# Attention visits of batch 1 half a step to a whole step later, in the middle of FFN steps and in the output steps

## The chip, the cores and the metric

One core of one Trainium2 chip. The metric is the device time of one execution in microseconds (us), the median over executions. Engines are named as in the profile: PE (TensorE matmul), PEld (its weight loads), DVE (VectorE), ACT (ScalarE), POOL (GpSimd), SP (SyncE, which here issues DMAs).

Where a time is compared with the kernel before, the ratio is the mean time of one kernel's runs over that of the other's of the same rounds, so it is not quite the ratio of the medians that are quoted.

## The reference, cut to what matters

```python
# attention with k and v projected from 1024 to 64 positions; 8 batches, 8 heads, head_dim 64
k_proj = einsum('ks,bhsd->bhkd', E, k);  v_proj = einsum('ks,bhsd->bhkd', F, v)
attn = softmax(q @ k_proj.T / sqrt(64)) ;  x = attn @ v_proj        # then heads are joined
# FFN on the 8192 x 512 tokens
h = maximum(maximum(x @ w1, x @ w2), x @ w3)                          # 512 -> 768
out = h @ w_out                                                       # 768 -> 512
```

## The kernel before

A batch is worked in two halves (`ch`, 512 tokens). One half is six FFN steps (`up`: three weights of four matmuls each give three PSUM banks, the tile `banks` into which PE writes its results; their maximum becomes one slice of `hT`) and four output tiles (`down`). PE always works on the FFN of batch b; the attention of batch b+1 is slipped in between steps as "visits", by a plan. The kernel is emitted in the written order on every engine, so the plan decides not only when PE does a visit but also where its Exp and Ln stand among the FFN's own ACT and DVE work.

```python
def two():    # two neighbouring PSUM banks; bank() deals one. The bank that a clock model says is free first
    ...
def sc(b, g):         # scores of a pair of heads: PE now, Exp on ACT at the next run_later()
    def f():
        t = scores(b, g, lo, nsi)
        later.append(lambda: exps(b, g, lo, nsi, t))

def za(b, g, then=False):        # PE: sums, values; ACT: Ln, then Exp(-x); DVE: xT = values * that
    def f():
        z = sums(b, g, lo, nsi)
        av = values(b, g, lo, nsi)
        invert(b, g, lo, nsi, z)             # zl = Ln (frees the sums' banks), zi = Exp
        ...
        scale_x(b, g, lo, nsi, av)           # xT
...
def up(b, ch, jt):
    h, done = [], []
    early = jt == 0
    for i in range(3):
        h.append(bank())
        up_mm(h[i][0], i, b, ch, jt, range(NCT - early))
        done.append(clock["pe"])
    ...
    h1s = ffn_sb.tile([P, CHUNK], FP32, name="h1s")
    nc.scalar.copy(out=h1s, in_=h[0][0])                       # ACT
    r = runs("s", done[0], 0.6, h[0][1])
    run_later()
    m12 = ffn_sb.tile([P, CHUNK], FP32, name="m12")
    nc.vector.tensor_tensor(out=m12, in0=h[1][0], in1=h1s, op=ALU.max)   # DVE
    runs("v", max(r, done[1]), 0.69, h[1][1])
    most(hTs[b, ch][:, jt, :], *h[2], m12)                     # DVE: hT
...
# plan of batch 0 (its visits are of batch 1), second half: (half, step); 6 to 9 are the output tiles
(1, 0): [kproj(1)],
(1, 1): [kt(1)],
(1, 2): [sc(1, 0), sc(1, 1), vproj(1), ld(2)],
(1, 3): [za(1, 0), sc(1, 2)],
(1, 4): [za(1, 1), sc(1, 3)],
(1, 5): [za(1, 2)],
(1, 7): [za(1, 3)],
...
for step in range(NJT):
    up(b, ch, step)
    behind(ch, step)           # the visits of (ch, step)
for tt in range(SPC):
    down(b, ch, tt, ...)
    behind(ch, NJT + tt)
```

`qT` of batch 1 is made by two DMA transposes issued on SP; the scores read it. The loads of k and v of batch 1 are issued by POOL near 24 and 26 us.

The softmax here doesn't subtract the row's maximum and nothing guards it: scores larger than these inputs give would overflow.

Of the kernel before, what the change touches and what calls it, by code (L numbers as in the profile page):

```python
# [15 lines left out]
def kernel(  # L16
# [62 lines left out]
    def bank():  # L79
        n = min(range(8), key=lambda n: free[n])  # L80
        deal((n,))
        return psum_t[:, n, :], (n,)
# [110 lines left out]
    def scores(b, g, lo, nsi):  # L193
        t, ns = two()
        n = nsi // 2
        for c in range(2):
            for hp in range(2):
                rows = slice(hp * HALF, (hp + 1) * HALF)
                at = g * SI + lo + c * n
                nc.tensor.matmul(  # L200
                    out=t[c * HALF:(c + 1) * HALF, hp, 0:n * P],
                    lhsT=kpTs[b][rows, g, :],
                    rhs=qTs[b][rows, at:at + n, :],
                    start=True, stop=True,
                )
        return t[:, :, 0:n * P], ns, pe(n * MM / 4 + 0.1)

    def exps(b, g, lo, nsi, sc):
        t, ns, ready = sc
        pTs[b, g, lo] = att.tile([P, 2, CHUNK], BF16, name="pT", bufs=4)[:, :, 0:nsi * HALF]  # L210
        nc.scalar.activation(out=pTs[b, g, lo], in_=t, func=AF.Exp, scale=scale)  # L211
        runs("s", ready, 0.17 + nsi * 0.107, ns)
# [14 lines left out]
    def sums(b, g, lo, nsi):  # L227
        return pair_mm(b, g, lo, nsi, lambda rows, hp: ones[rows])

    def invert(b, g, lo, nsi, z):  # L230
        t, ns, ready = z
        zl = att.tile([P, 2, CHUNK], FP32, name="zl", bufs=1)[:, :, 0:nsi * HALF]
        nc.scalar.activation(out=zl, in_=t, func=AF.Ln)  # L233
        runs("s", ready, 0.17 + nsi * 0.107, ns)
        if nsi == SI:
            zi = att.tile([P, 2, CHUNK], FP32, name="zi", bufs=2)
        else:
            zi = att.tile([P, 2, CHUNK // 2], FP32, name="zi0", bufs=4)
        nc.scalar.activation(out=zi, in_=zl, func=AF.Exp, scale=-1.0)  # L239
        zis[b, g, lo] = zi, runs("s", ready, 0.17 + nsi * 0.107)  # L240

    def values(b, g, lo, nsi):
        if b not in xTs:
            xTs[b] = att.tile([P, NCT, SI, P], BF16, name="xT")
        return pair_mm(b, g, lo, nsi, lambda rows, hp: vps[b][rows, 2 * g + hp, :])

    def scale_x(b, g, lo, nsi, av):
        t, ns, ready = av
        zi, when = zis.pop((b, g, lo))
        nc.vector.tensor_tensor(  # L250
            out=xTs[b][:, g, lo:lo + nsi, :].rearrange("a (c s) p -> a c (s p)", c=2),
            in0=t, in1=zi, op=ALU.mult,
        )
        runs("v", max(ready, when), 0.17 + nsi * 0.13, ns)
# [8 lines left out]
    def sc(b, g, lo=0, nsi=SI):  # L263
# [3 lines that stand above are left out]
        return f  # L267

    def za(b, g, lo=0, nsi=SI, then=False):
# [3 lines that stand above are left out]
            invert(b, g, lo, nsi, z)  # L273
            if then:
                later.append(lambda: scale_x(b, g, lo, nsi, av))
            else:
                scale_x(b, g, lo, nsi, av)
        return f
# [84 lines left out]
    def vproj(b):  # L363
        def f():
            t, ns = bank()
            proj(b, 2, t, (LO, HI), 4 * D)

            vps[b] = att.tile([P, H, D], BF16, name="vp")
            for hh, hs in enumerate((LO, HI)):
                i = t[hh * HALF:(hh + 1) * HALF, 0:4 * D].rearrange("a (h d) -> a h d", d=D)  # L370
                for to in range(2):
                    copy("sv"[hh], vps[b][to * HALF:(to + 1) * HALF, hs, :], i, ns, 0.4)
        return f
# [161 lines left out]
                most(hs[:, jt] if i == 1 else hTs[0, 0][:, jt, :], *h[jt], hs[:, jt])  # L535
                then((i, jt))

    def up(b, ch, jt):
        if jt == 0:
            hTs[b, ch] = ffn_sb.tile([P, NJT, CHUNK], BF16, name="hT")  # L540
        h, done = [], []
        early = jt == 0
        for i in range(3):
            h.append(bank())
            up_mm(h[i][0], i, b, ch, jt, range(NCT - early))
            done.append(clock["pe"])
        if early:
            for i in range(3):
                up_mm(h[i][0], i, b, ch, jt, (NCT - 1,))
                done[i] = clock["pe"]  # L550
        h1s = ffn_sb.tile([P, CHUNK], FP32, name="h1s")
        nc.scalar.copy(out=h1s, in_=h[0][0])  # L552
# [3 lines that stand above are left out]
        nc.vector.tensor_tensor(out=m12, in0=h[1][0], in1=h1s, op=ALU.max)  # L556
        runs("v", max(r, done[1]), 0.69, h[1][1])
        most(hTs[b, ch][:, jt, :], *h[2], m12)
# [50 lines left out]
    def ld(b):  # L609
        return lambda: load(b)  # L610

    def plan(b):
        n = b + 1
        if b == 0:
            c1 = (SPC, SPC)
            return {
                (0, 6): [za(0, 1, *c1), sc(0, 3, *c1)],
                (0, 7): [qd(1, 2), za(0, 2, *c1)],
                (0, 8): [za(0, 3, *c1)],
                (1, 0): [kproj(1)],  # L620
                (1, 1): [kt(1)],
                (1, 2): [sc(1, 0), sc(1, 1), vproj(1), ld(2)],
                (1, 3): [za(1, 0), sc(1, 2)],
                (1, 4): [za(1, 1), sc(1, 3)],
                (1, 5): [za(1, 2)],
                (1, 7): [za(1, 3)],
            }
        if b == 1:
            return {
                (0, 1): [qd(2)],  # L630
                (0, 5): [kproj(2), vproj(2), ld(3)],
                (0, 6): [kt(2)],
                (0, 7): [sc(2, 0)],
                (0, 9): [za(2, 0), sc(2, 1)],
                (1, 1): [za(2, 1), sc(2, 2)],
                (1, 3): [za(2, 2), sc(2, 3)],
                (1, 5): [za(2, 3)],
                (1, 6): [qd(3)],
            }
        if b == 2:  # L640
            return {
                (0, 2): [kproj(3), vproj(3), ld(4)],
                (0, 3): [kt(3)],
                (0, 4): [sc(3, 0)],
                (0, 6): [za(3, 0), sc(3, 1)],
                (1, 0): [za(3, 1), sc(3, 2), qd(4)],
                (1, 2): [za(3, 2), sc(3, 3), kproj(4), vproj(4), ld(5)],
                (1, 4): [kt(4)],
                (1, 5): [za(3, 3), sc(4, 0)],
            }  # L650
        if n == B:
            return {}
        out = {
            (0, 1): [za(n, 0), sc(n, 1)],
            (0, 3): [za(n, 1), sc(n, 2)],
            (0, 9): [za(n, 2), sc(n, 3)],
            (1, 3): [za(n, 3)],
        }
        if n + 1 < B:
            out[0, 6] = [qd(n + 1)]  # L660
            out[0, 9] += [kproj(n + 1), vproj(n + 1)]
            out[1, 1] = [kt(n + 1)]
            out[1, 3] += [sc(n + 1, 0)]
        if n + 2 < B:
            out[1, 1] += [ld(n + 2)]
        return out

    for b in range(B):
        p = plan(b)

        def behind(ch, step):
            for f in p.get((ch, step), []):
                f()

        for ch in range(NCHUNK):
            if (b, ch) == (0, 0):
                c1 = (SPC, SPC)
                up_first({
                    (0, 0, 5): [lambda: v_pair(2)],
                    (0, 1, 2): [lambda: x(2)],  # L680
                    (0, 1, 5): [lambda: v_pair(3), ld(1)],
                    (0, 2, 2): [lambda: x(3)],
                    (2, "a", 2): [qp(0, (0, 1), *c1)],
                    (2, "a", 4): [qp(0, (2, 3), *c1)],
                    (2, 0): [sc(0, 0, *c1)],
                    (2, 2): [sc(0, 1, *c1)],
                    (2, 4): [za(0, 0, *c1, then=True), sc(0, 2, *c1)],
                })
                run_later()
                behind(0, NJT - 1)  # L690
            else:
                for step in range(NJT):
                    up(b, ch, step)
                    behind(ch, step)
            for tt in range(SPC):
                down(b, ch, tt, "v" if (b, ch) == (0, 0) else "s")
                behind(ch, NJT + tt)
# [30 lines left out]
```

## Time and profile before

| | |
|---|---|
| time, median of 3 runs | 406.07 us (405.38 to 406.20) |
| span of the profiled run (this run took 406.83 us) | 405.1 us |
| PE / DVE / ACT busy | 97% / 49% / 47% |
| the stage that the change touches | 42.56 us |

The stage, used as a measure all through this document, goes from the start of the first matmul of batch 1's k projection to the start of the first matmul of batch 2's k projection on PE (49.15 and 91.71 us here). Both kernels do the same PE work between those two points, and the measure leaves out most of what differs from run to run while the first loads arrive. The landings of `qT` and v of batch 1 still fall inside it, and each stage is read from one profile, so a few tenths of a us between two stages are not yet a difference.

The page of the kernel before, its span and its first part:

```profile
span 405.1 us, 5869 instructions
PE 391.0 (97%) x2330; PEld 178.2 (44%) x2374; DVE 199.9 (49%) x309; ACT 190.9 (47%) x278; POOL 31.6 (8%) x44
```

The PE timeline of the kernel before. Columns: start, length, engine, source line, operation, output and inputs, shape, count; in brackets the idle time before the first one and what ended it. L496 is FFN weights, L284 the k and v projections, L200 scores, L220 sums and values, L591 output tiles.

```profile
52.86 2.75 PE L496 MATMUL banks<-xT,w_sb 128*128 128x512 bf16 x12
57.41 0.63 PE L200 MATMUL banks<-qT,kpT 64*64 64x512 bf16 x8 [1.80 <-DMA qT<-q_p]
57.97 1.06 PE L284 MATMUL banks<-v_t,efT 128*64 128x256 bf16 x16
...
62.12 0.81 PE L200 MATMUL banks<-qT,kpT 64*64 64x512 bf16 x4
62.85 2.76 PE L496 MATMUL banks<-xT,w_sb 128*128 128x512 bf16 x12
65.78 0.41 PE L220 MATMUL banks<-pT,ones 64*64 64x512 bf16 x4 [0.17 <-DVE xT L250]
66.00 0.41 PE L220 MATMUL banks<-pT,vp 64*64 64x512 bf16 x4
66.22 0.57 PE L200 MATMUL banks<-qT,kpT 64*64 64x512 bf16 x4
66.72 2.76 PE L496 MATMUL banks<-xT,w_sb 128*128 128x512 bf16 x11
69.66 0.41 PE L220 MATMUL banks<-pT,ones 64*64 64x512 bf16 x4 [0.18 <-DVE xT L250]
69.88 0.41 PE L220 MATMUL banks<-pT,vp 64*64 64x512 bf16 x4
70.22 2.76 PE L591 MATMUL banks<-wout_sb,hT 128*128 128x512 bf16 x12
...
73.47 2.76 PE L591 MATMUL banks<-wout_sb,hT 128*128 128x512 bf16 x12
76.08 15.70 PE L496 MATMUL banks<-xT,w_sb 128*128 128x512 bf16 x70
91.71 0.52 PE L284 MATMUL banks<-k_t,efT 128*64 128x256 bf16 x6
```

Three things are to be read here. The one large wait is 1.80 us on the transposed q. From 62 to 70 us there are several small waits. And the output tiles at 70 to 76 us follow each other without a wait on `hT`.

The lengths on PE must be read with care: ends are modelled (the Trainium skill, "Perfetto Trace Analysis", section "Tensor Engine Instruction (MATMUL, LD_WEIGHTS)", says so), and each record overlaps the next. Starts are safer. Between two starts, twelve 128x512 matmuls take 2.60 us in the stream (0.216 us each; the skill's "TensorE: Matmul & The Clock Gate", section "Wait — 56ns, not 53.3ns?", gives 215.7 ns, and the trace agrees), and 2.69 us where smaller tiles follow: 64x64 attention matmuls, or the 128x64 ones of a projection. So the wait on qT, from 52.86 + 2.69 = 55.55 to 57.41, is 1.86 us by starts; the bracket of 1.80 leaves out the modelled tail.

### The profile page before, as it was taken

The page shows a single profiled execution, that of the slowest core. Times are in us where ns is not written, and L with a number is a line of the kernel's source. Part 1 is how long each engine was busy: PE and PEld are TensorE (multiplying, and loading weights), DVE is VectorE, ACT ScalarE, POOL GpSimd, SP SyncE. Part 2 cuts the span into 40 slices and gives each one's busy share as a digit, 9 for nine tenths or more (in the row PEclk, how much of TensorE's full clock was granted, in tenths as well). Part 3 has the DMA queues.
Part 4 walks back from the last instruction along what each step waited for, and adds up shares of the span by engine and source line. Part 5 has one row for each costly group of instructions (what it writes and reads, how often), then busy time and mean ns, then how long its engine had stood idle before and what let it go on. Part 6 is the DMA issues. An engine that isn't in the chain of part 4 may idle for free.

```text
span 405.1 us, 5869 instructions
## 1 busy us (share of the span) xinstructions
PE 391.0 (97%) x2330; PEld 178.2 (44%) x2374; DVE 199.9 (49%) x309; ACT 190.9 (47%) x278; POOL 31.6 (8%) x44
## 2 busy tenths in 40 slices
PE   6899989999999999999999999999999999999996
PEld 3444433444444535444544445444544444444443
DVE  2348746462655527537353655626464363525251
ACT  2612429624763366555544555437535556432322
POOL 7440011002000100200200002000000000000000
PEclk9999999999999999999999999999999999999999
DMA  9999999949927994991898119950510202020202
GB/s 148 206 205 207 230 200 166 242 114 126 256 34 210 177 237 106 146 246 25 213 187 181 44 37 236 205 148 2 141 69 1 104 2 104 2 104 0 105 0 104
DMA packets 62667, 53.33 MB, mean 132 GB/s; under 512 B 30128, under 2 KB 58288, under 8 KB 62640
## 3 DMA queue, kind: packets, MB, share of 16 engines
q0 software_dynamic: 28512, 28.31, 44.0%
q1 hardware_dynamic: 33984, 24.51, 19.7%
q8 instruction: 18, 0.29, 0.3%
q10 hardware_dynamic: 144, 0.13, 0.1%
q14 instruction: 9, 0.07, 0.1%
HBM read 57.15 MB, written 16.78 MB: 183 GB/s over the span
## 4 chain that ended last, share of the span: by engine, by line
PE 83%; DMA 10%; ACT 2%; issue 1%; POOL 1%; DVE 1%; ACTq 0%; POOLq 0%
PE banks L496 55%; PE banks L591 19%; PE banks L220 4%; DMA q_t<-in_q_dram 3%; DMA qT<-q_p 3%; DMA w_sb<-in_moe_w_dram 3%; PE banks L284 3%; PE banks L200 2%; ACT pT L211 1%; ACT zl L233 1%; DVE xT L250 1%; ACT zi L239 1%; DMA out_dram<-o_sb 0%; POOL k_t L147 0%; POOL q_t L152 0%
## 5 line engine op out<-in xcount | busy, mean ns | idle before, releaser
L496 PE MATMUL banks<-xT,w_sb 128*128 128x512 bf16 x1118 | 254.7, 379 | 2.8 <-issue 0.6
L496 PEld LDWEIGHTS <-w_sb 128*128 128x128 bf16 x1152 | 109.5, 98 | 136.8 <-issue 9.8
L556 DVE TENSOR_TENSOR m<-banks,h1s 128x512 f32<-128x512 f32 x90 | 62.0, 689 | 85.1 <-ACT h1s L552 53.8
L552 ACT COPY h1s<-banks 128x512 f32<-128x512 f32 x90 | 52.4, 582 | 89.9 <-PE banks L496 87.2
L591 PE MATMUL banks<-wout_sb,hT 128*128 128x512 bf16 x370 | 84.8, 379 | 0.7 <-issue 0.3
L250 DVE TENSOR_TENSOR xT<-banks,zi 128x1024 bf16<-128x1024 f32 (+1 forms) x36 | 39.8, 1106 | 75.8 <-ACT zi L239 56.4
L506 DVE TENSOR_TENSOR hT<-banks,m 128x512 bf16<-128x512 f32 x90 | 62.3, 692 | 10.1 <-DVE m L556 0.5
L99 ACT COPY o_sb<-banks 128x512 f32<-128x512 f32 (+1 forms) x60 | 34.8, 580 | 53.0 <-PE banks L591 52.9
L591 PEld LDWEIGHTS <-hT 128*128 128x128 bf16 x378 | 36.0, 98 | 45.4 <-DVE hT L506 2.8
L233 ACT ACTIVATE zl<-banks 128x1024 f32<-128x1024 f32 (+1 forms) x36 | 33.5, 930 | 29.8 <-PE banks L220 28.9
L211 ACT ACTIVATE pT<-banks 128x1024 bf16<-128x1024 f32 (+1 forms) x36 | 33.2, 931 | 14.4 <-PE banks L200 14.4
L239 ACT ACTIVATE zi<-zl 128x1024 f32<-128x1024 f32 (+1 forms) x36 | 34.6, 962 | 1.1
L189 POOL DMA_DIRECT2D q_t<-in_q_dram x7 | 6.1, 878 | 204.1 <-DMA qT<-q_p 141.7
L200 PE MATMUL banks<-qT,kpT 64*64 64x512 bf16 (+1 forms) x144 | 13.7, 358 | 2.2 <-DMA qT<-q_p 1.8
L284 PEld LDWEIGHTS <-efT 128*64 128x64 bf16 x256 | 12.8, 110 | 5.0 <-issue 4.6
L220 PE MATMUL banks<-pT,ones 64*64 64x512 bf16 (+1 forms) x144 | 13.9, 376 | 0.8 <-DVE xT L250 0.3
L220 PE MATMUL banks<-pT,vp 64*64 64x512 bf16 (+1 forms) x144 | 13.3, 356 | 0.1
L99 DVE CAST vp<-banks 64x256 bf16<-64x256 f32 (+1 forms) x18 | 7.1, 396 | 9.3 <-ACT vp L99 5.9
L220 PEld LDWEIGHTS <-ones 64*64 64x64 bf16 x144 | 4.5, 103 | 14.6 <-issue 13.5
L99 ACT CAST vp<-banks 64x256 bf16<-64x256 f32 x14 | 5.1, 364 | 11.1 <-PE banks L284 10.9
L284 PE MATMUL banks<-k_t,efT 128*64 128x256 bf16 (+1 forms) x144 | 8.7, 263 | 1.3 <-DMA k_t<-in_k_dram 1.2
L99 DVE COPY q_p<-q_t 128x1024 bf16<-128x1024 bf16 x28 | 10.0, 420 | 0.0
(46 smaller groups left out, 96.7 us busy)
## 6 DMA issues: line engine op xcount, KB each, us to landing
out_dram<-o_sb SPq DMA_DIRECT2D x30, 512.0 KB, 2.9
q_t<-in_q_dram POOLq DMA_DIRECT2D x7, 1024.0 KB, 9.6
k_t<-in_k_dram POOLq DMA_DIRECT2D x7, 1024.0 KB, 13.8
v_t<-in_v_dram POOLq DMA_DIRECT2D x7, 1024.0 KB, 20.4
w_sb<-in_moe_w_dram POOLq DMA_DIRECT2D x5, 384.0 KB, 12.1
k_t<-in_k_dram POOLq DMA_DIRECT2D x2, 512.0 KB, 9.4
v_t<-in_v_dram POOLq DMA_DIRECT2D x4, 256.0 KB, 12.4
wout_sb<-in_moe_w_out_dram POOLq DMA_DIRECT2D x1, 768.0 KB, 16.3
```

The lines of the kernel that those rows point to most:

```text
L99: done = {"v": nc.vector.tensor_copy, "s": nc.scalar.copy, "g": nc.gpsimd.tensor_copy}[eng](out=o, in_=i)
L211: nc.scalar.activation(out=pTs[b, g, lo], in_=t, func=AF.Exp, scale=scale)
L220: nc.tensor.matmul(out=t[hp * HALF:(hp + 1) * HALF, c, 0:nsi * HALF], lhsT=w(rows, hp), rhs=p[rows, hp, :], start=True, stop=True,)
L233: nc.scalar.activation(out=zl, in_=t, func=AF.Ln)
L239: nc.scalar.activation(out=zi, in_=zl, func=AF.Exp, scale=-1.0)
L250: nc.vector.tensor_tensor(out=xTs[b][:, g, lo:lo + nsi, :].rearrange("a (c s) p -> a c (s p)", c=2), in0=t, in1=zi, op=ALU.mult,)
L284: nc.tensor.matmul(out=t[hh * HALF:(hh + 1) * HALF, 0:width], lhsT=efT[:, si, (kv - 1) * KP:kv * KP], rhs=qkv[b][kv][:, heads[hh], si, :], ...
L496: nc.tensor.matmul(out=h, lhsT=w_sb[i][:, ct, jt * P:(jt + 1) * P], rhs=xTs[b][:, ct, ch * SPC:(ch + 1) * SPC, :], start=(ct == first), st ...
L506: nc.vector.tensor_tensor(out=o, in0=h, in1=other, op=ALU.max)
L552: nc.scalar.copy(out=h1s, in_=h[0][0])
L556: nc.vector.tensor_tensor(out=m12, in0=h[1][0], in1=h1s, op=ALU.max)
L591: nc.tensor.matmul(out=o_ps, lhsT=hTs[b, ch][:, jt, tt * P:(tt + 1) * P], rhs=wout_sb[:, jt, :], start=(jt == 0), stop=(jt == NJT - 1),)
```

## The change

The intent: start batch 1's scores later, so that PE finds qT landed, and spread the visits out. The first two scores go from the end of step 2 to the middle of step 3 (after its second weight), with the v projection left behind at step 2; the next two visits go from the ends of steps 3 and 4 to the middles of steps 4 and 5; the last two go one step later, into the output tiles.

```diff
-    def up(b, ch, jt):
+    def up(b, ch, jt, mid=None):
...
             up_mm(h[i][0], i, b, ch, jt, range(NCT - early))
             done.append(clock["pe"])
+            if i == 1 and mid:
+                mid()
...
-                (1, 2): [sc(1, 0), sc(1, 1), vproj(1), ld(2)],
-                (1, 3): [za(1, 0), sc(1, 2)],
-                (1, 4): [za(1, 1), sc(1, 3)],
-                (1, 5): [za(1, 2)],
-                (1, 7): [za(1, 3)],
+                (1, 2): [vproj(1), ld(2)],
+                (1, (3, "mid")): [sc(1, 0), sc(1, 1)],
+                (1, (4, "mid")): [za(1, 0), sc(1, 2)],
+                (1, (5, "mid")): [za(1, 1), sc(1, 3)],
+                (1, 6): [za(1, 2)],
+                (1, 8): [za(1, 3)],
...
-                    up(b, ch, step)
+                    up(b, ch, step, lambda: behind(ch, (step, "mid")))
```

## The prediction

> **What bounds the kernel now.** TensorE. The page's first part has PE busy 391.0 of 405.1 us (97%), DVE 49%, ACT 47%; the chain of waits is 83% PE. In the only stage that the change touches (second half of batch 0) the view of waits has one large PE wait: 1.80 us, ended at 57.4 us by the DMA that transposes q of batch 1 (qT). From 57.41 to 76.08 us (PE timeline) it does some 16.9 us of work in 18.7 us (60 matmuls at 0.216 us start to start, four attention visits of about 0.75 us, the v projection 1.0 us); about 1.7 us go in small waits. ACT is busy 7.87 of the 8.3 us from 61.4 to 69.7 us (view of stretches): the softmax of batch 1 sets the pace there. At most about 3.5 us (0.9%) can be won.
>
> **What the change does.** It adds and removes no instruction; it reorders PE, ACT and DVE between about 55 and 78 us and deals PSUM banks differently after. With durations from the trace (128x1024 activations 0.96 to 1.03 us, h1s copy 0.5 to 0.58, xT scaling 1.23, maximum 0.69):
>
> 1. Gain: the first scores follow the v projection and eight more matmuls; qT has landed, the 1.8 us wait goes.
> 2. New DMA wait: the v projection now stands right after FFN step 2, where PE is ready at about 55.5 us. Its load was issued at 25.82 us and took 30.4 us to land (view of DMA issues): 56.2 us. About 0.8 us lost.
> 3. New waits on ACT order. A mid-step visit queues Ln and Exp (2 us) ahead of that step's h1s copy, and ACT works in order (the Trainium skill, "TensorE: Matmul & The Clock Gate", section "Architectural detail", says strict FIFO; the ACT timeline agrees). The visit at step 4 takes all banks that h1 and h2 leave, so its last scores wait for Ln to empty its pair: about 1.0 us; the third weight of step 5 likewise, about 0.5.
> 4. In step 5 h1s, the maxima and hT come after Ln, Exp and xT scaling of that visit; the first output tile's last matmul waits for that hT: about 1.7 us at some 70 to 72 us. Before, none.
> 5. The last visit is one output tile later, so batch 1's fourth xT slice is late by about 0.3 us.
> 6. The small waits of before at 62 to 70 us (1.4 us) go.
>
> My estimate chains these durations through the order and waits of both programs. For before it ends the stage at 76.06 us (trace 76.08); for after at about 77.0, plus item 5: a loss of 1.3 us, neither absorbed nor enlarged later.
>
> **Prediction.** 407.2 us; 405.5 to 408.6 should hold it 8 times in 10. Faster by over 2% 0.01, within 2% 0.97, slower by over 2% 0.02.
>
> **What would show each step.** Right: no PE wait on qT; about 0.8 us on the v load before the v projection; near 1 us on Ln at step 4's scores; about 1.7 us on hT before the last matmul of the first output tile; the next batch begins about 1 us after 76.1; PE busy time unchanged. Wrong: step 5's hT in time, or v already landed.
>
> **What would make it wrong.** If v lands earlier than in this trace, 0.8 us come back and the sum is near zero. If ACT keeps ahead better than the chained durations say, waits 3 and 4 shrink and the change gains up to 2 us. If the bank deal makes new waits in each later batch, it loses more.

## The result, and the profile after

Changed kernel: 407.64 us median of 4 runs (407.24 to 408.13), before in the same rounds 406.13; ratio 1.0041, 95% interval 1.0022 to 1.0059. Repeated on another occasion (below): 407.88 against 406.42, ratio 1.0029 (1.0011 to 1.0046). It is slower, by a third of a per cent, well inside 2%. The stage is 43.71 us (48.75 to 92.46), against 42.56.

The page of the changed kernel:

```profile
span 405.5 us, 5912 instructions
PE 394.5 (97%) x2374; PEld 178.0 (44%) x2374; DVE 200.2 (49%) x309; ACT 191.0 (47%) x278; POOL 31.5 (8%) x44
```

PE busy time rose by 3.5 us, but that says nothing: this trace holds all 2374 matmul records, the one of before 2330 of as many. The same changed kernel, profiled again (after_again below), shows 391.1 us with 2331 records. The stage is read from the PE timeline of the changed kernel:

```profile
52.46 2.75 PE L496 MATMUL banks<-xT,w_sb 128*128 128x512 bf16 x12
55.25 1.06 PE L284 MATMUL banks<-v_t,efT 128*64 128x256 bf16 x16
56.25 1.90 PE L496 MATMUL banks<-xT,w_sb 128*128 128x512 bf16 x8
58.08 0.63 PE L200 MATMUL banks<-qT,kpT 64*64 64x512 bf16 x8
...
61.57 0.39 PE L220 MATMUL banks<-pT,vp 64*64 64x512 bf16 x4
62.87 0.41 PE L200 MATMUL banks<-qT,kpT 64*64 64x512 bf16 x4 [0.91 <-ACT zl L233]
...
66.36 0.66 PE L200 MATMUL banks<-qT,kpT 64*64 64x512 bf16 x4
67.44 1.02 PE L496 MATMUL banks<-xT,w_sb 128*128 128x512 bf16 x4 [0.42 <-ACT zl L233]
68.30 1.24 PE L593 MATMUL banks<-wout_sb,hT 128*128 128x512 bf16 x5
71.18 0.39 PE L593 MATMUL banks<-wout_sb,hT 128*128 128x512 bf16 x1 [1.64 <-DVE hT L506]
...
76.62 15.91 PE L496 MATMUL banks<-xT,w_sb 128*128 128x512 bf16 x72
92.46 1.06 PE L284 MATMUL banks<-k_t,efT 128*64 128x256 bf16 x16
```

The wait on qT is gone (scores at 58.08, straight after the eight matmuls). In its place stand a wait of 0.91 and one of 0.42 us on Ln, and one of 1.64 us on `hT` before the last matmul of the first output tile, which before ran through (70.22). The chain of waits of the changed kernel shows how that last one comes about (columns: start, length, what):

```profile
66.36 1.03 ACT zl L233
67.40 0.02 issue
67.42 1.06 ACT zi L239
68.48 0.02 issue
68.51 1.23 DVE xT L250
69.73 0.61 DVE m L558
...
70.44 0.70 DVE hT L506
71.14 0.05 issue
71.18 0.39 PE banks L593
```

And the ACT timeline shows the copy that the FFN needed, behind the visit's two activations:

```profile
66.36 1.02 ACT L233 ACTIVATE zl<-banks 128x1024 f32<-128x1024 f32 x1 [1.06 <-PE banks L220]
67.42 1.06 ACT L239 ACTIVATE zi<-zl 128x1024 f32<-128x1024 f32 x1
68.38 0.57 ACT L554 COPY h1s<-banks 128x512 f32<-128x512 f32 x1
```

The h1 bank of step 5 was complete before the visit began, that is before 65.90 us; its copy starts at 68.38. ACT even sat idle for 1.06 us just before that Ln, while h1 was already there: the copy stands behind the visit in ACT's order, and ACT does not pass one piece of work ahead of another.

Why the scores wait for Ln: in the program's order, with bank numbers worked out from the output addresses, step 4 of the changed kernel is

```
h1 -> bank 2, h2 -> bank 4, (visit) sums -> 6,7  values -> 0,1  scores -> 6,7 [waits for Ln of the sums], h3 -> bank 5
```

The core has eight PSUM banks (the skill, "PSUM — Partial Sum Buffer", section "Specifications (TRN2)"; the dealt numbers here run from 0 to 7). h1 and h2 hold two banks, the visit wants six, the third weight one. What counts is pairs: h1 and h2 lie in two different pairs (2,3 and 4,5), so only two whole pairs were left for the three that the visit wants. The scores got the sums' own pair, which only Ln frees. At step 5 the third weight got bank 0, also one of the sums' pair: the 0.42 us. The scores of step 5 got banks 4 and 5, and bank 5 was still held by step 4's h3 until its `hT` was made (66.55 us), so their group took 0.66 us instead of the 0.41 of an unhindered one: 0.25 us that the prediction did not have.

The account of the stage, all by starts (0.216 us a matmul of the stream, 2.69 us for twelve followed by smaller tiles, 0.24, 0.22 and 0.31 us for sums, values and scores):

| term of the prediction | predicted, us | measured, us | from |
|---|---|---|---|
| wait on qT goes | -1.8 | -1.86 | 55.55 to 57.41 before |
| wait for the v load comes | +0.8 | +0.10 | 52.46 + 2.69 = 55.15 to 55.25 |
| waits on Ln, steps 4 and 5 | +1.5 | +1.60 | 61.79 to 62.87 and 66.92 to 67.44 |
| step 5's scores wait for step 4's hT | none | +0.25 | 0.66 against 0.41 us |
| wait on hT at the first output tile | +1.7 | +1.80 | 68.30 + 5 x 0.216 = 69.38 to 71.18 |
| fourth xT slice late | +0.3 | +0.21 | 72 matmuls take 15.84 us, before 15.63 |
| small waits at 62 to 70 us go | -1.4 | -1.10 | 0.42, 0.24, 0.19 and 0.25 us before |
| sum | +1.1 | +1.00 | the stage grew by 1.15 |

The prediction's own chained estimate was 1.3 us; its terms as listed add up to 1.1.

About 0.15 us of the stage is not assigned; some 0.1 of it would be one more change from full-array matmuls to smaller ones (2.69 instead of 2.60 us), which comes with the eight matmuls between v projection and scores. After the stage nothing was lost: from 91.71 us to the end are 313.4 us before, from 92.46 us 313.0 us in the changed kernel. The timed difference of 1.5 us (interval of the ratio: 0.9 to 2.4 us) agrees with the stage.

### The profile page after: what moved, and what is told of

The parts are those of the page before. It is cut to its first block, busy times and chain, and to the rows that moved or that the text cites. A ratio compares the mean times of both kernels' runs of the same rounds, so it can differ in the third digit from the quotient of the medians.

```text
span 405.5 us, 5912 instructions
## 1 busy us (share of the span) xinstructions
PE 394.5 (97%) x2374; PEld 178.0 (44%) x2374; DVE 200.2 (49%) x309; ACT 191.0 (47%) x278; POOL 31.5 (8%) x44
## 4 chain that ended last, share of the span: by engine, by line
PE 90%; DMA 4%; ACT 2%; DVE 2%; POOL 1%; issue 1%; DVEq 0%; ACTq 0%; POOLq 0%
PE banks L496 61%; PE banks L593 19%; PE banks L220 4%; PE banks L284 3%; DMA w_sb<-in_moe_w_dram 3%; PE banks L200 2%; DVE xT L250 1%; ACT zl L233 1%; ACT zi L239 1%; DMA out_dram<-o_sb 0%; ACT pT L211 0%; POOL k_t L147 0%; POOL q_t L152 0%; POOL v_t L147 0%; DVE m L558 0%
## 5 line engine op out<-in xcount | busy, mean ns | idle before, releaser
L496 PE MATMUL banks<-xT,w_sb 128*128 128x512 bf16 x1152 | 258.0, 379 | 1.6 <-DMA w_sb<-in_moe_w_dram 1.0
L593 PE MATMUL banks<-wout_sb,hT 128*128 128x512 bf16 x378 | 85.7, 379 | 1.6 <-DVE hT L506 1.6
L284 PEld LDWEIGHTS <-efT 128*64 128x64 bf16 x256 | 12.8, 110 | 4.7 <-issue 3.6
L380 PE MATMUL banks<-warm 128*128 128x512 bf16 x24 | 8.8, 497 | 1.2 <-DVE warm L170 1.2
```

The source lines that it names most:

```text
L284: nc.tensor.matmul(out=t[hh * HALF:(hh + 1) * HALF, 0:width], lhsT=efT[:, si, (kv - 1) * KP:kv * KP], rhs=qkv[b][kv][:, heads[hh], si, :], ...
L496: nc.tensor.matmul(out=h, lhsT=w_sb[i][:, ct, jt * P:(jt + 1) * P], rhs=xTs[b][:, ct, ch * SPC:(ch + 1) * SPC, :], start=(ct == first), st ...
L593: nc.tensor.matmul(out=o_ps, lhsT=hTs[b, ch][:, jt, tt * P:(tt + 1) * P], rhs=wout_sb[:, jt, :], start=(jt == 0), stop=(jt == NJT - 1),)
```

## The experiments

The theory: the time is lost to the order of work on two in-order engines. A visit in the middle of a step puts its Ln and Exp on ACT ahead of that step's h1s copy, and its xT scaling on DVE ahead of that step's maxima. Rivals: the v projection's new place makes PE wait for the v load; the later last visits make batch 1's x late; the new dealing of banks harms later batches. Eight kernels ran in two groups of four, each group on one chip with its own runs of the kernel before (medians 406.42 and 406.32 us). All gave correct results.

### after_again: the changed kernel as it is

No edit.

> The changed kernel once more, as the control of this group on one chip. Both theories: 0.2 to 0.5% slower than before. Measure for all runs: the stage, from the first matmul of batch 1's k projection to the first matmul of batch 2's k projection on PE: 42.56 us before, 43.71 us changed; expected again 43.4 to 44.4.

Measured: 407.88 us, ratio 1.0029 (1.0011 to 1.0046), stage 43.82 us (48.19 to 92.01), the same waits of 0.91, 0.43 and 1.64 us. The loss is repeatable and sits in the same places.

### act_order: h1s ahead of the visit on ACT

```diff
-            if i == 1 and mid:
+            if i == 1 and mid and not early:
+                h1s = ...; nc.scalar.copy(out=h1s, in_=h[0][0]); r = runs("s", done[0], 0.6, h[0][1])
                 mid()
...
-        h1s = ...; nc.scalar.copy(out=h1s, in_=h[0][0]); r = runs(...)
+        if early or not mid:
+            h1s = ...; nc.scalar.copy(out=h1s, in_=h[0][0]); r = runs(...)
         run_later()
```

(In this and every kernel with the early copy, `mid` is passed only to the three steps that have a mid-step visit.)

> The changed kernel with one thing undone: in a step that has a mid-step visit, the h1s copy is put on ACT ahead of the visit's Exp and Ln instead of behind them. Theory (order on ACT and DVE in the visits of steps 4 and 5 costs the time): the 0.9 us wait for Ln at step 4's scores goes, but hT of step 5 still stands behind the xT scaling on DVE, so the PE wait before the last matmul of the first output tile stays at about 1.5 us; stage shorter by about 0.8 us than the changed kernel's, 42.6 to 43.3, time about the same as before. Rival (the v load and the later last visits cost the time, ACT order does not): stage as the changed kernel's, 43.4 to 44.4.

Measured: 406.46 us, ratio 1.0007 (0.9987 to 1.0028), stage 42.71 us. The Ln waits on PE are gone; the wait on hT is still 1.15 us (about 1.5 was expected). Small waits on DVE (0.4 and 0.2 us) appeared at step 5's scores. The edit also changes the bank deal: with h1 copied early, step 4's scores get banks 2 and 3, the pair of h1, and no longer the sums' pair. The Ln wait goes for this reason, although Ln itself now stands behind the copy. In the stage 1.0 to 1.1 us came back, and no difference from the kernel before is left that the interval could tell. By the stage, the rival that ACT's order does not matter is out; the time alone would not settle it, since its interval overlaps that of after_again. This half alone brings no gain.

### act_dve_order: also the xT scaling behind that step's hT on DVE

```diff
+    # za(..., end=True): scale_x is kept in a list `last` ...
-                (1, (4, "mid")): [za(1, 0), sc(1, 2)],
-                (1, (5, "mid")): [za(1, 1), sc(1, 3)],
+                (1, (4, "mid")): [za(1, 0, end=True), sc(1, 2)],
+                (1, (5, "mid")): [za(1, 1, end=True), sc(1, 3)],
...
         most(hTs[b, ch][:, jt, :], *h[2], m12)
+        for f in last: f()
+        last.clear()
```

> As act_order, and the xT scaling of the visits of steps 4 and 5 is put on DVE behind that step's hT instead of ahead of it. The visits stay where the change put them. Theory: the PE wait on hT at the first output tile goes too, stage shorter by about 2.9 us than the changed kernel's, 40.5 to 41.4, and the kernel is 0.3 to 0.5% faster than before. Rival: stage 43.4 to 44.4, 0.2 to 0.5% slower than before.

Measured: 405.04 us, ratio 0.9965 (0.9949 to 0.9982), stage 40.44 us (48.81 to 89.25), just below the expected range. The visits are where the change put them, and the kernel is faster than before. The first output tile on its PE timeline now runs through, with six matmuls in a row and no wait:

```profile
65.82 0.82 PE L498 MATMUL banks<-xT,w_sb 128*128 128x512 bf16 x3
66.70 1.46 PE L602 MATMUL banks<-wout_sb,hT 128*128 128x512 bf16 x6
68.08 0.41 PE L220 MATMUL banks<-pT,ones 64*64 64x512 bf16 x4
```

and on its DVE timeline the maxima of step 5 stand ahead of the visit's scaling:

```profile
65.37 0.69 DVE L564 TENSOR_TENSOR m<-banks,h1s 128x512 f32<-128x512 f32 x1 [0.16 <-PE banks L220]
66.90 0.69 DVE L508 TENSOR_TENSOR hT<-banks,m 128x512 bf16<-128x512 f32 x1 [0.83 <-PE banks L200]
67.58 1.23 DVE L250 TENSOR_TENSOR xT<-banks,zi 128x1024 bf16<-128x1024 f32 x1
```

This settles the main question: with the places of the change kept, only the two orders altered, 3.3 us of stage come back. The v projection and the last visits stand where they stood, so neither of those rivals carries the loss.

### score_mid_only: the first scores moved, the four visits where they were

```diff
                 (1, 2): [vproj(1), ld(2)],
                 (1, (3, "mid")): [sc(1, 0), sc(1, 1)],
-                (1, (4, "mid")): [za(1, 0), sc(1, 2)],
-                (1, (5, "mid")): [za(1, 1), sc(1, 3)],
-                (1, 6): [za(1, 2)],
-                (1, 8): [za(1, 3)],
+                (1, 3): [za(1, 0), sc(1, 2)],
+                (1, 4): [za(1, 1), sc(1, 3)],
+                (1, 5): [za(1, 2)],
+                (1, 7): [za(1, 3)],
```

> Half of the change alone: the v projection right after step 2 and the first two scores in the middle of step 3, the four visits at the places they had before (ends of steps 3, 4, 5 and second output tile). Theory: the gain without the cost; no PE wait on qT, none over 0.5 us on hT; stage 41.3 to 42.1, 0.1 to 0.35% faster than before. Rival (the new wait for the v load eats the gain): stage 42.4 or more, no faster than before.

Measured: 405.22 us, ratio 0.9975 (0.9956 to 0.9995), stage 41.37 us. The half of the change that removes the qT wait is a gain, even though v landed late in this profile (it also waited 0.33 us for the k load just before the stage begins, which the stage leaves out): the PE timeline has

```profile
56.23 1.06 PE L284 MATMUL banks<-v_t,efT 128*64 128x256 bf16 x16 [0.43 <-DMA v_t<-in_v_dram]
```

### dve_order: the DVE half alone

The edit of act_dve_order without that of act_order.

> The changed kernel with only the DVE half of the repair: the xT scaling of the visits of steps 4 and 5 goes behind that step's hT on DVE, while on ACT Exp and Ln stay ahead of the h1s copy. Theory: the two orders work in series, hT of step 5 still waits for h1s behind Ln and Exp, so this alone wins only some 0.4 to 0.9 us of stage (from 43.7 to 42.8 to 43.3) and the Ln wait of 0.9 us at step 4's scores stays; time within 0.25% of before. Rival (DVE order alone is the cause, ACT order is not): stage at most 41.6, as with both halves (the run with both was 0.35% faster than before).

Measured: 407.79 us, ratio 1.0031 (1.0019 to 1.0043), stage 43.37 us. Both numbers miss the expectation on the slow side, the stage by 0.07 us, and the time shows no gain. The hT wait shrank to 0.63 us, but step 5's scores now wait 1.29 us for Ln, where in the changed kernel the third weight waited 0.42 us:

```profile
69.05 0.41 PE L200 MATMUL banks<-qT,kpT 64*64 64x512 bf16 x4 [1.29 <-ACT zl L233]
...
72.14 0.39 PE L598 MATMUL banks<-wout_sb,hT 128*128 128x512 bf16 x1 [0.63 <-DVE hT L508]
```

What follows: the rival that DVE's order alone is the cause is out. The two halves are in series. In the program's order of this kernel step 5's sums go to banks 6 and 7 and its scores to the same pair, as at step 4 (in the changed kernel the scores of step 5 still had a pair of their own, 4 and 5). The program deals the banks itself when it is built, and the place of the scaling is the only difference of the two programs, so the other deal is this edit's doing. Part of the 1.29 us stays open: Ln starts 0.84 us after the first of the sums (67.14 to 67.97), in the changed kernel 0.46 us after it, and the trace does not show why.

### no_mid5: only step 5's visit back at the step's end

```diff
-                (1, (5, "mid")): [za(1, 1), sc(1, 3)],
+                (1, 5): [za(1, 1), sc(1, 3)],
```

> The changed kernel with only the visit of step 5 put back to the end of that step, behind its third weight; the visits of steps 3 and 4 stay in the middle. Theory: no hT wait of 1.6 us at the first output tile's last matmul; the Ln wait of 0.9 us at step 4 stays; waits of about 0.6 us in all move to the third visit; stage shorter by about 1.2 us, 42.2 to 42.9; time equal to before within 0.2%. Rival (the waits come from all mid-step places alike or from the later last visits): stage shorter by less than 0.5 us.

Measured: 406.31 us, ratio 1.0003 (0.9990 to 1.0017), stage 42.24 us, 1.5 us shorter than the changed kernel's. The hT wait is gone, the 0.91 us on Ln at step 4 is still there, and waits of 0.36 and 0.38 us appeared at the third visit. One visit in one place made about the whole net loss (the changed kernel did not run in this group, so this rests on the stage and on the return to the time of before): the step before the output tiles is the one whose `hT` is needed at once.

### v_first: the kernel before with the v projection ahead of the scores

```diff
-                (1, 2): [sc(1, 0), sc(1, 1), vproj(1), ld(2)],
+                (1, 2): [vproj(1), ld(2), sc(1, 0), sc(1, 1)],
```

> The kernel before with one swap: the v projection of batch 1 stands ahead of its first two scores instead of behind them; nothing else moves. It measures what the qT wait alone is worth. Theory: the wait on qT shrinks from 1.8 us to 0.3 to 1.0 us, a wait for the v load of 0 to 0.8 us may come; stage shorter than before by about 1.0 us (41.3 to 42.0), 0.1 to 0.35% faster. Rival (the softmax chain on ACT sets the stage's length and takes the gain back): stage 42.3 or more, no faster than before.

Measured: 405.37 us, ratio 0.9973 (0.9960 to 0.9986), stage 41.05 us, 1.5 us shorter than before. The wait on qT is 0.21 us. Both are a little better than the expected ranges. So a shorter qT wait is really worth its time on PE, and this one-line swap is not told apart from score_mid_only by their intervals; the ACT chain behind it did not take the gain back. `qT` also landed earlier after its issue here than in the profile of before (12.2 against 12.8 us), so some of the 1.5 us is that; the timed gain is 1.1 us.

### ad_vmid: both orders repaired, and the v projection in the middle of step 3

```diff
# on top of act_dve_order
-                (1, 2): [vproj(1), ld(2)],
-                (1, (3, "mid")): [sc(1, 0), sc(1, 1)],
+                (1, (3, "mid")): [vproj(1), ld(2), sc(1, 0), sc(1, 1)],
```

> The kernel with both orders repaired (h1s ahead on ACT, xT scaling behind hT on DVE), and the v projection put into the middle of step 3, just ahead of the scores, so that eight matmuls stand between step 2 and it. If the v load's landing still holds PE (0.2 us seen in the changed kernel, 0.4 us with scores alone in the middle), the stage is shorter by up to 0.8 us than with both orders repaired and the kernel is 0.4 to 0.65% faster than before; if v lands in time, no difference to that kernel (0.25 to 0.45% faster than before).

Measured: 404.12 us, ratio 0.9952 (0.9936 to 0.9967), stage 40.24 us. No wait for v is left, although the load took 30.5 us from issue to landing here. Against act_dve_order's stage the gain is 0.2 us, but this profile waited 0.25 us for the k load just before the stage begins, which the stage leaves out; both spans are 402.3 us, and the two ratios' intervals overlap (they are of two chips). So a gain over act_dve_order is not shown. (The 0.2 us that the text above names for the changed kernel is 0.1 by the account given here.) This kernel is faster than both the kernel before and the changed one.

## Why the prediction was right

It said 407.2 us with a range of 405.5 to 408.6; measured were 407.64 and 407.88. Point by point:

- **What bounds the kernel.** Right. Changes of the stage by PE waits (40.24 to 43.82 us) came out in the time with the same sign, within about 0.7 us of the same size, and outside the noise, for all but act_order and no_mid5, which were meant to be equal. One part of it no run shows: that the softmax on ACT "sets the pace there". With the qT wait gone in both and the same work on ACT, act_dve_order's stage is 0.9 us shorter than that of score_mid_only, which keeps the visits' old places.
- **Gain of the qT wait.** Right: -1.86 us by starts, and v_first shows that it is worth taking.
- **The v load.** The term that was mis-sized: predicted 0.8 us, measured 0.10. The estimate took the landing at 56.2 us from the one trace of before; in the changed kernel's trace v landed at 55.2 us. From issue to landing the same 1 MB load took 29.0 to 30.5 us over the ten profiles, in two groups: 30.4 to 30.5 in before, score_mid_only and ad_vmid (where the transposes of q took 12.8 us), 29.0 to 29.7 in the other seven (10.3 to 12.3). What makes a profile fall in one or the other is not known. So before's stage is one with late landings and the changed kernel's one with early landings: had before's first transpose taken 12.2 us, its qT wait would have been some 0.6 us shorter (an estimate from these traces) and the stage difference larger than 1.15. The timed ratios do not rest on this.
- **ACT order and banks.** Right in mechanism and place; the two Ln waits were 1.60 us instead of 1.5. The 0.25 us on step 4's hT was not foreseen. act_order removes the Ln waits.
- **hT of the last step.** Right: 1.80 against 1.7 us, at 69.4 to 71.2 us. no_mid5 and act_dve_order remove it in two different ways.
- **Late xT slice.** Right, 0.21 against 0.3 us. No run moves the last visit alone, but in all seven profiles with the later visit those 72 matmuls take 15.84 us and in the other three 15.63 to 15.64.
- **Small waits of before.** Right in kind; 1.10 us instead of 1.4.
- **Nothing later.** Right: 313.0 to 313.4 us from the end of the stage to the end of the span in all profiles. The rival that the new deal harms later batches is out; inside the stage the deal is part of the cause, as said.
- **"PE busy time unchanged"** as a check was a poor choice: the page shows +3.5 us only because the trace of before lacks 44 matmul records.

That the number came so close is partly luck: the v load was put 0.7 us too high, the other terms together 0.6 us too low, and the two nearly cancelled.

The prediction also named the way to a gain, "if ACT keeps ahead". act_dve_order brings that about by emission order, and the gain is 1.4 us.

## What to carry to other kernels

Moving work to a later place on the bottleneck engine also moves its followers on the in-order engines behind it: before placing a visit inside a step, emit what the step itself still needs (here the copy and the maxima) ahead of the visit's followers, and check both engines: the ACT half alone brought the time back to that of before, the DVE half alone returned 0.3 us of the stage, both together let the gain of the change show. Be strictest at the last step before a consumer that has no slack. Count the PSUM banks at the point of the visit: here two held banks in two different pairs left too few pairs, and the scores waited 1.08 us for an activation to free one.

## What the Trainium skill lacked or had wrong

- "TensorE: Matmul & The Clock Gate", section "Back-to-back issue gap": it gives about 131 ns per 128x128x512 matmul as the sustained spacing in a stream of weight load and matmul pairs and says that the 216 ns formula over-counts. The runs show 0.216 us: twelve such pairs in 2.60 us from start to start (49.74 to 52.34 us in the changed kernel).
- The same page, "Part 3: Packing small matmuls — row/col tiling", gives no figure for what it costs to go from full-array matmuls to smaller tiles, and no other page read has one. Twelve matmuls take 2.60 us when small transposes on the full array follow and 2.69 us when 64x64 attention matmuls or a 128x64 projection follow, so about 0.1 us at each such change.
- "Perfetto Trace Analysis", section "Tensor Engine Instruction (MATMUL, LD_WEIGHTS)", says that ends on PE are modelled; it does not say that gaps read from them come out short. The three brackets of 1.80, 0.91 and 1.64 us are 1.86, 1.08 and 1.80 us by starts.
- "Perfetto Trace Analysis" does not tell that some matmul records can be missing from a trace: 44 of 2374 in the profile of before, none in that of the changed kernel, so PE busy times of two traces are not comparable (the changed kernel itself shows 394.5 us with all its records and 391.1 with 2331).
- No page read for this case has the spread of a load's landing: the same 1 MB load took 29.0 to 30.5 us in ten profiles.
